# Asking for one part of a quarter's keys a block earlier, in a kernel that fills one queue with loads

## The chip, the core and the metric

The kernel runs on 1 core of one Trainium2 chip. What counts is the device time of one execution in microseconds (us), as the median of several runs. The engines are TensorE (PE in the profile: matmuls; PEld: its weight loads), VectorE (DVE), ScalarE (ACT), GpSimd (POOL) and SyncE (SP), which issues every DMA of this kernel on one queue.

## What is computed

For one sequence of 2048 rows and 512 columns the kernel computes a sliding-window attention with 32 heads of 16 columns and a dense layer with a gelu, and mixes the two by a gate:

```python
S, D, F, H, Dh, W = 2048, 512, 1792, 32, 16, 256
q, k, v = heads(x @ wqkv)
scores = einsum("bhqd,bhkd->bhqk", q, k) * Dh ** -0.5
mask = (idx[:, None] - idx[None, :] >= 0) & (idx[:, None] - idx[None, :] < W)
a = (softmax(where(mask, scores, -1e9)) @ v) @ wo
b = gelu(x @ w1 + b1) @ w2 + b2
g = sigmoid((x * gate_w).sum(-1, keepdims=True))
out = g * a + (1 - g) * b
```

## The kernel before, in words

The rows are cut into four quarters of 512 (T), a quarter into four blocks of 128 keys (NB = 4). The heads are worked on in eight groups of four. So attention runs over 8 x 16 = 128 blocks (NU), that is 32 quarters, one after the other. Every product is made of float32 values split into a high and a low part, hence three matmuls for one (`mm3`, L127 to L129).

First come the projections of all four quarters; their queries and keys go to DRAM (SQ and SK, in high and low parts). Then attention runs, interleaved on TensorE with the dense layer: the matmuls `u` (x times w1) and `y` (times w2) in eight pieces (`mlp`), and at the end `a` (times wo).

Attention has two passes, the second twelve blocks behind the first (LEAD = 12):

- The maxima. `att_max` (L667, its matmul is L680, called sm after its output) multiplies 64 queries of the tile `qd` with the 320 keys of the tile `kd` that their window covers, and VectorE takes the largest (L684). `kd` has two slots, for quarters in turn. A slot holds 256 + 512 keys: first the last 256 of the quarter behind (the old part), then the quarter's own 512 (the new part). Half block j of a quarter (j from 0 to 7) reads the 320 keys that end at 64(j+1) + 256.
- The scores. `att_exp` (L724, matmul L736, called st) multiplies keys in `ks` with queries in `qs`, and ScalarE takes the exponential (L765). At each quarter's end `att_pvs` multiplies with the values (L792, pv_sm and pv_st).

All loads go through `send` (L138), that is SP's queue, in the order in which the program text is run. `load_kd` (L639) sends the old part from SK of the quarter behind and the new part from SK of the quarter itself; `load_qd`, `load_ks` send three DMAs each, `load_qs` two, `att_load_v` one. SP runs its queue in order. A DMA is issued when the tile it overwrites has been read, when what it reads is written, and when the DMA eight issues before has landed, as eight semaphores go round.

The order of all instructions is written out by a planner in the kernel's own text. It keeps a clock with a cost for each step. `send` books 500 ns (ISSUE) of a line and one of eight lanes for 5 or 7 us (LOADS, SLOW); `arrive` (L149) marks a key such as ("qd", group, quarter) with the booked landing plus 1.2 us. `scores` (L1202) yields for each step the keys that it needs, and the loop behind it (L1249) then takes the attention step, or a matmul of the dense layer, by what is marked ready. The planner does not see the chip: where its clock is off, engines wait.

In `scores`, m counts the blocks of the maxima and u = m - 12 those of the scores. At the second step (i == 1) of the first block of a quarter (m % 4 == 0) the loads of the next quarter of maxima are asked for: `kd`, old part and new, then `qd`. In this same block, at its end, follow `ks` for the next quarter of scores (as 12 is a multiple of 4) and the values. `qs` is asked for at the end of the second block of a quarter of maxima at first, then at that of the third. The dense layer adds its own: `load_x` (L882) brings the next quarter of x as four DMAs called `mx`, in a tile (tag xt) of which there is one buffer; at the end of the first `u` the last quarter's x is stored from that tile (XT<-xt).

Of the kernel before, what the change touches and what calls it, by code (L numbers as in the profile page):

```python
# [19 lines left out]
NT = S // T  # L20
NB = T // 128
# [11 lines left out]
def gated_mix(ctx: ExitStack, tc: tile.TileContext, x, wqkv, wo, w1, b1, w2, b2, gate_w, out):  # L33
# [12 lines left out]
    def f32(ap):  # L46
        return ap.bitcast(F32)
# [90 lines left out]
    def send(to, by, ns=LOADS):  # L138

        nc.sync.dma_start(to, by)  # L140
        k = sent[0] = (sent[0] + 1) % 8
        at = max(line[0], now[0], lanes[k])
        line[0], lanes[k] = at + ISSUE, at + ns
# [5 lines left out]
    def arrive(key):  # L149

        mark(key, lanes[sent[0]] + MARGIN)

    def after(ns, fn, *args):
        now[1] += 1
        heapq.heappush(todo, (now[0] + ns, now[1], fn, args))
# [353 lines left out]
    def qkv(t):  # L509
# [38 lines left out]
        for n, (kind, j) in enumerate(pieces):  # L548
# [18 lines left out]
            if t == 2 and n in (1, 2):  # L567
                load_kd(0, n - 1)
# [25 lines left out]
    def repeat():  # L594

        t, j, to, by = twice.pop(0)
        send(to, by)
        mark(("twice", t, j))
# [3 lines left out]
    def slot(g_, c):  # L602
        return (g_ * NT + c) % 2

    def heads(st, g_):

        return st[g_ // 4][2 * (g_ % 4):2 * (g_ % 4) + 2]

    def ready(t, g_, k):
        need(*[(("qk", "twice")[g_ // 4], t, k * NC + 2 * (g_ // 4) + a) for a in range(2)])  # L610
# [5 lines left out]
    def load_ks(g_, c):  # L616


        ready(c, g_, 1)
        n = 2 * NB  # L620
        put_pairs([f32(ks[64 * s + 4:64 * s + 52, slot(g_, c)]) for s in range(2)], SK[c], g_)
        arrive(("ks", g_, c))

    def put_pairs(to, st, g_):

        n = 2 * NB
        for s in range(2):
            v = to[s].rearrange("r a x -> r (a x)")
            src = part(st, g_, s)
            if s:  # L630
                mid = v[:, 192:192 + 256 * (n - 1)].rearrange("r (n x) -> r n x", x=256)[:, :, 0:128]
                send(mid, src[:, 64:64 + 128 * (n - 1)].rearrange("r (n x) -> r n x", x=128), SLOW)
                ends = v.rearrange("r (n j) -> r n j", j=64)[:, 0:4 * n:4 * n - 1]
                send(ends, src.rearrange("r (n j) -> r n j", j=64)[:, 0:2 * n:2 * n - 1], SLOW)
            else:
                v = v.rearrange("r (n x) -> r n x", x=256)[:, :, 64:192]
                send(v, src.rearrange("r (n x) -> r n x", x=128), SLOW)

    def load_kd(g_, c):  # L639
        for t in range(max(c - 1, 0), c + 1):  # L640
            ready(t, g_, 1)
            k0 = 0 if t == c else T - W
            at = W if t == c else 0
            src = heads(SK[t], g_)[:, :, :, :, k0:].rearrange("s d u a c -> (s d u) a c")
            send(f32(kd[0:96, slot(g_, c), :, at:at + T - k0]), src, SLOW)

    def load_qd(g_, c):
        ready(c, g_, 0)
        put_pairs([f32(qd[48 * s:48 * s + 48, slot(g_, c)]) for s in range(2)], SQ[c], g_)
        arrive(("qd", g_, c))  # L650

    def load_qs(g_, c):
        ready(c, g_, 0)
        need(("v", NT - 2, NB - 1))
        for s in range(2):
            v = f32(qs[64 * s + 4:64 * s + 52, :, c * T:(c + 1) * T])
            send(v, part(SQ[c], g_, s).rearrange("r (a c) -> r a c", a=2))
        arrive(("qs", g_, c))

    def att_load_v(g_, c):  # L660
        need(*[("v", c, b) for b in range(NB)])
        vt = vbuf[:, c % 2]
        dst = vt[:, 0:NB * 68].rearrange("p (j c) -> p j c", c=34)
        send(dst, SV[c].rearrange("p j s c -> p (j s) c")[:, :, 34 * g_:34 * g_ + 34])
        vts[g_, c] = vt

    def att_max(g_, b, i):  # L667

        if b % RB == 0 and (g_, b // RB) not in Ms:
            Ms[g_, b // RB] = sb.tile([128, 2 * RB, 2], F32, tag="M", bufs=2, name=f"M{g_}_{b}")  # L670
        M = Ms[g_, b // RB]
        hb, pr = divmod(i, 2)
        c, n = b // NB, slot(g_, b // NB)
        j = 2 * (b % NB) + hb
        w = min(64 * (2 * b + hb + 1), W + 64)
        k1 = 64 * (j + 1) + W
        bank("sm", ("max", g_, b, i))
        p = ps.tile([128, 320], F32, tag="sm", bufs=3, name=f"sm{g_}_{b}_{i}")
        v = pairs(p[:, :w])
        nc.tensor.matmul(v, qd[0:96, n, pr, 128 * j:128 * (j + 1)], two(kd[0:96, n, pr, k1 - w:k1]),  # L680
                         start=True, stop=True)

        def red():
            nc.vector.tensor_tensor_reduce(v, v, two(mask[:, 320 - w:320]), 1.0, -3e38,  # L684
                                           ALU.add, ALU.max, M[:, 2 * (b % RB) + hb, pr:pr + 1])
        tick(max(w / 2.4 + 6, 110))
        put("V", w / 0.96 + 117, red, 130, 500, key=("max", g_, b, i))

    def att_rows(g_, rb):
        def turn():  # L690
            turn_of(g_, rb)

        def puts():
            for i in range(4):
                for hb in range(2):
                    put("G", 400, lambda i=i, hb=hb: put_rows(g_, rb, i, hb), PUT * (i + 0.5 * hb), 1500,
                        key=("rows", g_, rb) if i == 3 and hb else ("row", g_, rb, i, hb))
        put("V", 720, turn, 0, 1500, key=("turn", g_, rb), then=puts,
            req=[("v", NT - 2, NB - 1)] + [("max", g_, rb * RB + b, i) for b in range(RB) for i in range(4)])
# [18 lines left out]
    def rows_of(g_, kb, i):  # L718

        k0 = kb * 128 + i // 2 * 64  # L720
        w = min(W + 64, S - k0)
        return [("rows", g_, b) for b in range(kb // RB, (k0 + w - 1) // (RB * 128) + 1)]
# [47 lines left out]
    def blocks_of(kb):  # L770

        return list(range(max(kb - 5, 0), kb + 1))
# [422 lines left out]
    NU = NG * NKB  # L1195
# [6 lines left out]
    def scores():  # L1202

        for u in range(-LEAD, NU):
            m = u + LEAD
            gm, bm = divmod(m, NKB)
            step_ = STEP if u >= 0 else STEP0
            for i in range(4):
                if i == 1 and m % NB == 0 and NB <= m < NU - NB:
                    load_kd(*divmod(m // NB + 1, NT)), load_qd(*divmod(m // NB + 1, NT))  # L1210
                if i % 2 == 0:
                    pair = (i, i + 1) if stage[0] != "u" else (i,)
                elif len(pair) == 2:
                    continue
                else:
                    pair = (i,)
                for op, i in [(op, k) for k in pair for op in ORDER[:3]] + [("f", k) for k in pair]:
                    if op == "s" and u >= 0:
                        yield (rings["st"][0], ("ks", u // NKB, u % NKB // NB), *rows_of(u // NKB, u % NKB, i))
                        att_exp(u // NKB, u % NKB, i)  # L1220
                    if op == "m" and m < NU:
                        yield (rings["sm"][0], ("qd", gm, bm // NB))
                        att_max(gm, bm, i ^ XOR)
                    if op == "p" and i == PVAT and 1 <= u <= NU - LEAD and u % NB == 0:
                        g_, kb = divmod(u - 1, NKB)
                        yield (rings["st"][0], rings["sm"][0], *[("pt", g_, b, h) for b in blocks_of(kb) for h in (0, 1)])
                        att_pvs(u - 1)
                    if op == "f":
                        yield step_ / 4
            if m < NU and bm % RB == RB - 1:  # L1230
                att_rows(gm, bm // RB)
            if m % NB == QAT % NB and QAT <= m < QAT + NKB:
                load_qs(0, (m - QAT) // NB)
            if u > NU - LEAD and u % NB == 0:
                yield ()
                att_pvs(u - 1)
            if u % NB == 0 and NB <= u < NU - NB:
                load_ks(*divmod(u // NB + 1, NT))
            if u % NB == 2 and NB < u < NU - 3 * NB:
                load_qs(*divmod(u // NB + 3, NT))  # L1240
            if COPY[0] <= u < COPY[1] and u % 2 == 1 and twice:
                repeat()
            if u % NB == 0 and u >= 0:
                att_load_v(*divmod(u // NB, NT))
            if u - NU + NKB == YAT:
                for k in range(6):
                    after(1500 + YGAP * k, load_y, *divmod(k, 2))
# [94 lines left out]
```

## Time and profile before

| | |
|---|---|
| median of 3 runs | 703.48 us (703.24 to 703.89) |
| the profiled execution | 704.36 us |
| its span, first to last instruction | 702.4 us |
| TensorE busy | 691.5 us, 98% of the span |
| granted TensorE clock | 1.000 |
| first and last load of kd | at 80.9 and 585.0 us |

The profile is of one execution. Times in it count from the span's start. A chain of waits is followed back from the last instruction, at each step to what released it. A row of the timeline has start, length, engine, line (L140 is the issue in `send`), operation, out<-in and how many instructions of one kind follow one another; where several follow, the length takes in the waits between them. The waits view says who waited for whom: us in all, how often, the longest.

### The profile page before, as it was taken

To read this page: it belongs to the slowest core of one execution; us is meant where nothing else is said; L and a number is where in the kernel's file an instruction comes from. 1 tells how busy PE (TensorE), PEld (TensorE's weight loads), DVE (VectorE), ACT (ScalarE), POOL (GpSimd) and SP (SyncE) were. 2 spreads that over 40 slices of the span, in tenths; PEclk is the share of its full clock that TensorE was granted. 3 is DMA by queue.
4 is the path that set the end of the run, shared out by engine and by line. 5 is a ranking of instruction groups with operands and counts; after the bars stand their busy time and mean duration, and the time that the engine had idled before them with its cause. 6 is when DMAs were issued, how large, how long until landed. Compare 5 with 4: busy or idle time off the path is not lost.

```text
span 702.4 us, 17477 instructions
## 1 busy us (share of the span) xinstructions
PE 691.5 (98%) x6129; PEld 594.1 (85%) x6129; DVE 514.4 (73%) x1558; ACT 416.5 (59%) x972; POOL 364.9 (52%) x855
## 2 busy tenths in 40 slices
PE   8999999999899999999999999999999999999998
PEld 7888888888688888888888888888888888878886
DVE  4733326799769977986898799869878986984653
ACT  4434532369438845863696488449746954894641
POOL 4200000569756865786589667757865776630000
PEclk9999999999999999999999999999999999999999
DMA  9979698999898899799997799997999899757652
GB/s 309 367 229 386 201 403 244 287 315 249 218 265 189 211 286 246 176 234 256 293 229 186 219 247 220 248 271 176 253 244 241 178 220 293 204 167 219 201 201 100
DMA packets 178102, 169.97 MB, mean 242 GB/s; under 512 B 56544, under 2 KB 122848, under 8 KB 178016
## 3 DMA queue, kind: packets, MB, share of 16 engines
q1 hardware_dynamic: 178016, 168.87, 87.1%
q8 instruction: 48, 0.79, 0.5%
q14 instruction: 38, 0.31, 0.2%
HBM read 111.68 MB, written 61.34 MB: 246 GB/s over the span
## 4 chain that ended last, share of the span: by engine, by line
PE 85%; DMA 7%; DVE 2%; ACT 2%; issue 1%; POOL 1%; SPq 1%; POOLq 0%; DVEq 0%; ACTq 0%
PE sm L680 9%; PE st L736 8%; PE pv_sm L792 7%; PE y L127 6%; PE y L129 6%; PE y L128 6%; PE u L127 6%; PE u L128 5%; PE u L129 5%; PE qk L127 4%; PE qk L129 4%; PE qk L128 4%; PE a L127 2%; PE a L129 2%; PE a L128 2%; PE v L127 2%
## 5 line engine op out<-in xcount | busy, mean ns | idle before, releaser
L684 DVE CUSTOM_DVE_ANT_1 sm<-sm,mask 128x320 f32<-128x320 f32 (+4 forms) x512 | 230.4, 489 | 62.2 <-PE sm L680 58.2
L752 POOL TENSOR_SCALAR_AFFINE_SELECT pt<-pt 64x256 f32<-64x256 f32 (+1 forms) x538 | 208.9, 408 | 110.6 <-ACT pt L765 99.7
L765 ACT ACTIVATE pt<-st 128x320 f32<-128x320 f32 (+4 forms) x512 | 191.9, 427 | 108.3 <-PE st L736 105.0
L680 PE MATMUL sm<-kd,qd 96*128 96x320 f32 (+4 forms) x512 | 148.0, 304 | 1.0 <-DVE M L684 0.8
L736 PE MATMUL st<-qs,ks 128*128 128x320 f32 (+4 forms) x512 | 143.1, 297 | 2.9 <-DMA ks<-SK 1.7
L716 POOL CAST qs<-tt 4x256 fp32r<-4x256 f32 x256 | 123.9, 484 | 27.5 <-DVE tt L708 15.9
L680 PEld LDWEIGHTS sm<-kd,qd 96*128 96x128 f32 x512 | 96.8, 189 | 19.9 <-DVE M L684 5.7
L736 PEld LDWEIGHTS st<-qs,ks 128*128 128x128 f32 x512 | 97.3, 190 | 11.6 <-issue 2.3
L129 PE MATMUL y<-w2h,h 128*128 128x512 f32 x224 | 85.1, 380 | 0.8 <-DVE h L961 0.5
L127 PE MATMUL y<-w2h,h 128*128 128x512 f32 x224 | 85.1, 380 | 0.0
L128 PE MATMUL y<-w2l,h 128*128 128x512 f32 x224 | 84.8, 378 | 0.0
L127 PE MATMUL u<-mx,w1h 128*128 128x512 f32 x196 | 76.9, 393 | 0.2 <-DVE sqh L949 0.2
L129 PE MATMUL u<-mx,w1l 128*128 128x512 f32 x196 | 74.3, 379 | 0.0
L128 PE MATMUL u<-mx,w1h 128*128 128x512 f32 x196 | 74.2, 379 | 0.0
L792 PE MATMUL pv_sm<-pt,vbuf 64*32 64x320 f32 (+4 forms) x1408 | 73.3, 346 | 0.1
L792 PE MATMUL pv_st<-pt,vbuf 64*32 64x320 f32 (+4 forms) x1408 | 72.9, 346 | 0.0
L684 DVE DVE_READ_ACCUMULATOR2_ANT M<- 128x1 f32 x512 | 71.2, 139 | 0.0
L792 PEld LDWEIGHTS pv_sm<-pt,vbuf 64*32 64x32 f32 x1408 | 49.4, 106 | 22.2 <-issue 3.2
L456 DVE TENSOR_TENSOR qke<-qk,qke 128x512 fp32r<-128x512 f32 x32 | 22.1, 691 | 40.9 <-ACT qke L453 31.3
L453 ACT ACTIVATE qke<-qk 128x512 fp32r<-128x512 f32 x32 | 19.1, 598 | 51.5 <-PE qk L129 28.6
L129 PEld LDWEIGHTS y<-w2h,h 128*128 128x128 f32 x224 | 42.2, 188 | 7.3 <-DVE h L961 1.3
L473 POOL MEMSET vx<- 128x32 f32 x16 | 2.4, 154 | 85.9 <-DMA SQ<-qke 32.0
(165 smaller groups left out, 1331.8 us busy)
## 6 DMA issues: line engine op xcount, KB each, us to landing
kd<-SK SPq DMA_DIRECT2D x32, 384.0 KB
qs<-SQ SPq DMA_DIRECT2D x64, 192.0 KB
mx<-XT SPq DMA_DIRECT2D x24, 512.0 KB
SQ<-qke SPq DMA_DIRECT2D x16, 512.0 KB
SK<-qke SPq DMA_DIRECT2D x16, 512.0 KB
ND<-nd SPq DMA_DIRECT2D x32, 256.0 KB
raw_w<-in_B_w_dram SPq DMA_DIRECT2D x28, 256.0 KB
qd<-SQ SPq DMA_DIRECT2D x32, 192.0 KB
```

Source lines behind the costliest of these rows:

```text
L127: nc.tensor.matmul(p, lh, rh, start=first, stop=False)
L128: nc.tensor.matmul(p, lh, rl, start=False, stop=False)
L129: nc.tensor.matmul(p, ll, rh, start=False, stop=last)
L453: nc.scalar.activation(halves(e[:, h]), p, AF.Copy)
L456: nc.vector.tensor_sub(halves(e[:, 1 - h]), p, halves(f32(e[:, h])))
L680: nc.tensor.matmul(v, qd[0:96, n, pr, 128 * j:128 * (j + 1)], two(kd[0:96, n, pr, k1 - w:k1]), start=True, stop=True)
L684: nc.vector.tensor_tensor_reduce(v, v, two(mask[:, 320 - w:320]), 1.0, -3e38, ALU.add, ALU.max, M[:, 2 * (b % RB) + hb, pr:pr + 1])
L716: nc.gpsimd.tensor_copy(dst, src.unsqueeze(1).broadcast_to([4, 2, RB, 32]))
L736: nc.tensor.matmul(pairs(p[:, :w]), ks[:, slot(g_, kb // NB), pr, at:at + 128], two(qs[:, pr, k0:k0 + w]), start=True, stop=True)
L752: nc.gpsimd.affine_select(out=v, in_=v, pattern=[[0, v.shape[1]], [1 - 2 * e, 64]], compare_op=ALU.is_ge, fill=0.0, base=-e, channel_multi ...
L765: nc.scalar.activation(halves(pt[:, hf, pr, :w]), sorted_(p[:, :w]), AF.Exp, scale=SCALE)
L792: nc.tensor.matmul(pv[r // 64][32 * i:32 * i + 32, q - c * T:e - c * T], vts[g_, b // NB][r:r + 64, v:v + 32], rhs(r), start=start, stop=s ...
```

## The change

`load_kd` gets two switches for its two parts. The old part of quarter n + 2 is asked for in the last block of quarter n (m % 4 == 3), at the second step; the new part and `qd` stay where both parts and `qd` were, at the second step of the block that follows.

```diff
-    def load_kd(g_, c):
-        for t in range(max(c - 1, 0), c + 1):
+    def load_kd(g_, c, old=True, new=True):
+        for t in range(c - 1 if old and c else c, c + new):
             ready(t, g_, 1)
             k0 = 0 if t == c else T - W
             at = W if t == c else 0
...
             for i in range(4):
+                if i == 1 and m % NB == NB - 1 and m < NU - 2 * NB:
+                    load_kd(*divmod(m // NB + 2, NT), new=False)
                 if i == 1 and m % NB == 0 and NB <= m < NU - NB:
-                    load_kd(*divmod(m // NB + 1, NT)), load_qd(*divmod(m // NB + 1, NT))
+                    load_kd(*divmod(m // NB + 1, NT), old=False), load_qd(*divmod(m // NB + 1, NT))
```

The first quarter of each group has no quarter behind it and so no old part.

## The prediction

> **What bounds the kernel now.** I read the page of the profile first, then who TensorE waited for, then the SyncE (SP) queue around the one large wait, and last the DMA engines' share there.
>
> ```profile
> span 702.4 us, 17477 instructions
> ...
> PE 691.5 (98%) x6129; PEld 594.1 (85%) x6129; DVE 514.4 (73%) x1558; ACT 416.5 (59%) x972; POOL 364.9 (52%) x855
> ```
>
> TensorE is busy for 691.5 of 702.4 us, so everything that is not a matmul can give back at most 702.4 - 691.5 = 10.9 us, over the whole span. The change adds and removes no matmul. The second full resource is the DMA, in the view of its queues and issues:
>
> ```profile
> DMA packets 178102, 169.97 MB, mean 242 GB/s; under 512 B 56544, under 2 KB 122848, under 8 KB 178016
> ...
> q1 hardware_dynamic: 178016, 168.87, 87.1%
> ...
> kd<-SK SPq DMA_DIRECT2D x24, 192.0 KB
> ```
>
> One queue's packets take 87.1% of the 16 engines' span; the old parts of `kd` are 24 transfers of 192 KB in it. The change moves loads, so the question is whether a load ends any of those 10.9 us. The view of waits, kept to TensorE, answers it:
>
> ```profile
> engine line waited for: us in total, times, longest us
> PE st L736 <- DMA ks<-SK: 1.7, 1, 1.7
> PE warm0.0_188 L506 <- POOL idle L57: 1.2, 1, 1.2
> ...
> PE st L736 <- ACT nd L812: 0.8, 1, 0.8
> PE sm L680 <- DVE M L684: 0.8, 2, 0.5
> ```
>
> One DMA stands in it: once, for 1.7 us, a score matmul (st) waited for the load of `ks`. The matmuls of the maxima (sm), which are the readers of `kd`, waited for VectorE only. The same from the other side, the view of the tile `kd`:
>
> ```profile
> L140 SPq DMA_DIRECT2D kd<-SK x56: 540/569/2288, 80.9 to 585.0; - x56
> ...
> its engine sat idle before it (us, times) until:
>   DVE M L684: 6.5, 21
>   issue: 4.3, 22
> ```
>
> Before 512 weight loads and 512 matmuls on `kd`, no idle time ended with the landing of a `kd` or `qd` load. So the transfer that is moved is on no path today. Its first-order worth is nil, and what is left are side effects: on the loads behind it in SP's queue, on the full DMA engines, and on the order that the planner writes.
>
> **The change part by part.** Calls first. `scores` asks for the old part at every m = 3, 7, ... up to 119 (30 calls); the seven that belong to quarter 0 of a group have no old part and issue nothing. So 23 DMAs are moved, one to a quarter, each by one block of keys; none is added or removed, bytes are the same.
>
> *SP's issue slots.* At the median of 569 ns from the row above, 23 x 0.569 = 13.1 us of issuing leave the bursts at the quarters' starts and stand elsewhere in the same queue. In sum SP does the same. What that frees depends on whether SP was the late one at the burst. Two places show both answers; first a quarter in the steady state, then the narrow window inside its pair of `kd` loads:
>
> ```profile
> 227.95 5.17 SPq L140 DMA_DIRECT2D kd<-SK  x2
> 233.17 1.76 SPq L140 DMA_DIRECT2D qd<-SQ  x3
> 235.03 1.72 SPq L140 DMA_DIRECT2D ks<-SK  x3
> ```
>
> ```profile
> 232.58 0.55 SPq L140 DMA_DIRECT2D kd<-SK  x1
> ```
>
> The columns are start, length, what. The old part goes out at 227.95; the new part only at 232.58, and between them SP stands for about 232.58 - 227.95 - 0.57 = 4.1 us, because the new part overwrites keys that the quarter's last maxima still read. The old part's own region, the first 256 keys, is read by the first two blocks of a quarter only (the window of half block j ends at 64(j+1)+256 and is 320 wide, so it leaves these keys from j = 4 on). It has no such wait, neither here nor one block sooner. Here the old part's slot is covered by the wait that follows; taking it away lets `qd` and `ks` start at the same 233.17 and 235.03. Worth 0.
>
> The change adds no wait for TensorE at the new place: at block 3 of the quarter the readers, blocks 0 and 1, are done by a whole block. What SP can meet there is the landing of the DMA eight issues back, since eight semaphores go round:
>
> ```profile
> SPq L140 <- DMA kd<-SK: 29.5, 31, 1.8
> ```
>
> Such waits for a `kd` load come to 29.5 us in 31 places, none over 1.8 us. They are moved with it rather than removed: the queue holds eight whatever their order. Queued behind the moved issue are then the parts of `mx`, `ya`, `ND` and the copies of SQ and SK that fall between the block and the quarter's end, and after them the new part of `kd`, `qd` and `ks`. Who waits for those: TensorE for none of the first kind (no row of the waits above), so up to 1.8 us plus a 0.57 us slot is hidden there by loads that land before they are needed. If that cover is gone, the bill is those 2.4 us at one place.
>
> *The one place where a load ends the wait of TensorE.* The chain that ended last runs through it:
>
> ```profile
> 164.94 7.08 DMA kd<-SK
> 172.04 7.75 DMA XT<-xt
> ...
> 182.31 4.29 DMA ks<-SK
> 186.60 0.09 issue
> 186.69 0.37 PE st L736
> ```
>
> and SP's queue over the same time:
>
> ```profile
> 160.95 3.26 SPq L140 DMA_DIRECT2D qs<-SQ  x2
> 164.31 0.53 SPq L140 DMA_DIRECT2D raw_w<-in_B_w_dram  x1
> 164.94 1.45 SPq L140 DMA_DIRECT2D kd<-SK  x2
> 166.44 1.75 SPq L140 DMA_DIRECT2D qd<-SQ  x3
> 168.85 4.39 SPq L140 DMA_DIRECT2D XT<-xt  x4
> 179.94 0.32 SPq L140 DMA_DIRECT2D mx<-XT  x1
> 180.31 2.46 SPq L140 DMA_DIRECT2D ks<-SK  x3
> ```
>
> To be read: the old part of `kd` issues at 164.94 and lands at 172.02; it is the eighth before the fourth store of `xt`, which therefore goes out at 172.04 and lands at 179.79; the first part of `mx` overwrites `xt`, so SP stands until 179.94; `ks` stands behind `mx` in the queue, lands at 186.60, and the matmul starts at 186.69. At first sight the moved load begins this chain, and its early departure should pull all of it forward. But how far can it go? One block sooner in the queue puts it behind the two `qs` (asked at the end of the block two before), so its issue can start at 160.95 + 3.26 = 164.21 at the soonest, not at 164.94: 0.73 us. And the fourth store then waits for another of the same four predecessors (two `qs`, the weight, the old part), which go through the same engines. Those were full:
>
> ```profile
> 160.00:165.00 5.00, 5.00 (x29) 4.28 (x28) 5.00 (x20) 5.00 (x13) 4.74 (x9) 1.00 1.10 188
> 165.00:170.00 5.00, 5.00 (x57) 4.26 (x63) 4.86 (x20) 5.00 (x14) 4.78 (x11) 1.00 1.07 241
> 170.00:175.00 5.00, 5.00 (x75) 4.35 (x59) 5.00 (x11) 4.78 (x11) 4.60 (x10) 1.00 1.11 320
> ```
>
> The last two columns are the DMA engines' share and GB/s. At 1.10, 1.07 and 1.11 the engines have no gap, and a permutation of what waits in front of them ends at the same moment. So this term lies between -0.73 us (the whole shift arrives) and 0 (only the order changes); it could be above 0 only by the planner's order, which is priced below. I take 0, by the shares.
>
> [...]
>
> *The planner's clock.* `send` books 500 ns of line per issue (ISSUE, L143) and one of eight lanes for 7 us (SLOW); `arrive` marks `qd` and `ks` from these. With one issue fewer in the burst these marks come about one ISSUE sooner, more where a lane was booked out. From the second quarter on the order of dense and attention matmuls on TensorE can therefore differ, by a matmul here and there. That costs nothing by itself, as TensorE has the same work and 98% fill. It is unknown in sign: the waits of TensorE beside the startup are 0.8 us and less apiece, so I bound the sum by one wait of the largest size seen, 1.7 us, each way.
>
> *The sum.* 0 (slots) + 0 (kd's own readers) + 0 (the chain at 186.69, bound -0.73) + 0 (order, bounds -1.7 and +1.7). The profiled execution took 704.36 us, its span 702.4 and 1.96 around it, and is 0.88 above the median of the runs, 703.48; the change comes out as a difference of 0, so the forecast is **703.5 us** by the median. A measurement of this kernel can tell about 0.2%, 1.4 us, from no change.
>
> **The rivals.**
>
> *The load does not really go sooner.* SP is late at many bursts (at 164 us it works off a backlog: 3.26 us for two `qs`), so an instruction placed one block sooner leaves the chip a few tenths sooner. For it: the 0.73 us above. Against: in the steady quarter SP passes the old part at 227.95, well ahead of the new one, so there it is on time. The result is also 703.5 us.
>
> *The wait at 186.69 goes.* If the planner's earlier marks put `ks` ahead of the `xt` stores and `mx`, or more dense matmuls ahead of that st, TensorE no longer stands there: 703.48 - 1.73 = 701.8 us. The 1.73 is this row's:
>
> ```profile
> 186.69 0.37 PE L736 MATMUL st<-qs,ks 128*128 128x320 f32 x1 [1.73 <-DMA ks<-SK]
> ```
>
> For it: it is the only wait for a load, and the moved DMA is in its chain. Against: the chain's middle, the stores and the 7 us of SP behind them, has nothing to do with `kd`, and it would need 1.4 of 1.73 us to go where I find at most 0.73.
>
> *A longer wait at a quarter's first st (slower).* The planner now believes that `ks` lands sooner; the chip, with full DMA engines, does not land it sooner. Where the mark of `ks` decides when attention goes on, the st comes sooner in TensorE's order, with fewer dense matmuls ahead of it, and TensorE, which runs in order, stands for the rest. In the place above the st is at the landing already, so each dense matmul that changes to behind it adds its own time, 0.22 us by the step of this chain:
>
> ```profile
> 157.60 0.22 PE u L127
> ```
>
> From seven of them on (7 x 0.22 = 1.5 us) it is a measurable loss; with eight, 1.7 us (703.48 + 1.7), the result is 705.2 us. For it: the boundary has no slack, and nothing on the chip holds the planner to the truth. Against: the mark moves by about 500 ns, which is two or three such matmuls, unless a booked lane adds to it.
>
> **How the numbers follow.** Forecast (moved, covered) 0.38; not really sooner 0.14; both within 0.2%, together 0.52. The wait goes 0.24, at 701.8. A new or longer wait 0.24, at 705.2. The range takes in both side cases' centres, since leaving either out leaves more than 2 in 10 outside: 701.7 to 705.3; it leaves about 0.2 for tails beyond. The likeliest case's own range is 702.7 to 704.4. Chances: faster 0.24, same 0.52, slower 0.24.
>
> **What would show it right or wrong.** In the changed kernel the pair of `kd` loads at a quarter is one, the other stands about a block (some 4 us) sooner; TensorE's busy time stays at 691 to 692 us; the waits of TensorE for VectorE and ScalarE stay near today's; sm still waits for no DMA. The forecast holds by its reasons if the wait of st for `ks` near 187 us is there again within 0.7 us of 1.7, and no second DMA stands in the view of TensorE's waits. It is wrong towards faster if that row is gone and the idle time of TensorE is down from 10.9 to about 9; wrong towards slower if a row for `ks`, `kd`, `qd` or `mx` of over a microsecond has come.

## The result

The changed kernel takes 710.73 us by the median (710.31 to 713.04), the kernel before 703.68 us beside it. The ratio is 1.011, with a 95% interval of 1.0091 to 1.013: it is slower by 7 us, outside the range of the forecast. Beside the experiments below the kernel before took 700.5 to 709.0 us, with medians of 702.45 to 703.65, so each run there is told by its ratio to the kernel before beside it, with the 95% interval. The profiled execution of the changed kernel took 713.04 us. Its page and its longest waits of TensorE:

```profile
span 710.6 us, 17479 instructions
...
PE 695.5 (98%) x6129; PEld 597.1 (84%) x6129; DVE 518.7 (73%) x1560; ACT 417.7 (59%) x972; POOL 361.1 (51%) x853
```

```profile
engine line waited for: us in total, times, longest us
PE sm L680 <- DVE M L684: 4.0, 5, 2.1
PE y L129 <- DVE h L961: 2.2, 2, 1.2
PE u L127 <- DVE sqh L949: 2.1, 3, 0.9
PE warm0.0_188 L506 <- POOL idle L57: 1.2, 1, 1.2
PE st L736 <- ACT nd L812: 0.9, 1, 0.9
```

Two rows of the kernel before that go with it:

```profile
PE u L127 <- DVE sqh L949: 0.6, 2, 0.4
PE y L129 <- DVE h L961: 0.5, 1, 0.5
```

The span grew by 8.2 us (702.4 to 710.6): idle time of TensorE from 10.9 to 710.6 - 695.5 = 15.1 us, and its busy time by 4.0 us. No DMA stands in TensorE's waits any more: the row of `ks` is gone. The three rows for VectorE (sm, y and u) were 1.9 us before and are 8.3 us now, each for the result of a matmul that VectorE has not yet read or finished. So no load holds TensorE up in this execution, and it is worse off.

The load itself left sooner, but mostly by less than a block. SP's queue at the quarter shown before, first the row that stood just ahead of the pair of `kd` loads at 227.95 in the kernel before, then the changed kernel:

```profile
227.26 0.59 SPq L140 DMA_DIRECT2D SK<-SK  x1
```

```profile
231.58 0.55 SPq L140 DMA_DIRECT2D kd<-SK  x1
232.17 0.60 SPq L140 DMA_DIRECT2D SK<-SK  x1
237.06 0.55 SPq L140 DMA_DIRECT2D kd<-SK  x1
237.65 1.76 SPq L140 DMA_DIRECT2D qd<-SQ  x3
239.51 1.71 SPq L140 DMA_DIRECT2D ks<-SK  x3
```

The old part leaves at 231.58, 5.5 us ahead of the new one. But in the kernel before it was 232.58 - 227.95 = 4.6 us ahead already: SP had come to it early, so here the old part only changes places with one copy of SK and gains 0.9 us. Over the 23 moved loads its lead on the new part grew from 0.7 us to 3.1 us at the median. The new part waits for TensorE as it did before (4.3 us, before 4.1). `qd` and `ks` follow the new part with the same spacing as before. The `kd` readers of the changed kernel:

```profile
L140 SPq DMA_DIRECT2D kd<-SK x56: 539/552/1195, 81.3 to 595.0; - x56
...
its engine sat idle before it (us, times) until:
  DVE M L684: 14.4, 26
  issue: 3.8, 19
```

Idle time that VectorE ended has grown from 6.5 to 14.4 us (weight loads and matmuls together), and still none of it ends with a load.

Where the time went shows in two stretches, taken from the table of busy times. Columns: stretch, its length, busy time of TensorE, its weight loads, VectorE, ScalarE and GpSimd, then the granted clock, the DMA share and GB/s. Before:

```profile
130.00:200.00 70.00, 66.86 (x493) 57.27 (x493) 58.73 (x193) 43.21 (x96) 51.46 (x101) 1.00 0.98 261
340.00:450.00 110.00, 109.58 (x1126) 92.31 (x1125) 98.08 (x311) 79.73 (x186) 81.56 (x184) 1.00 0.92 229
```

After:

```profile
130.00:200.00 70.00, 64.93 (x469) 54.83 (x468) 55.47 (x177) 40.41 (x88) 47.68 (x91) 0.98 0.87 245
340.00:450.00 110.00, 106.55 (x1032) 90.67 (x1036) 100.07 (x317) 80.42 (x187) 80.33 (x180) 1.00 0.90 223
```

Between 130 and 200 us, where the scores begin, TensorE is idle for 5.1 us and not 3.1; between 340 and 450 us for 3.4 us and not 0.4. In the second stretch the kernel before left TensorE next to no gap while VectorE was busy for 89% of the time. A part of the 8.2 us is the clock, an estimated 1.7 us: in this execution TensorE's granted clock was about 0.50 for 3.4 us (last section).

### The profile page after: what moved, and what is told of

Same layout as the page of the kernel before. It is cut to its first block, busy times and chain, and to the rows that moved or that the text cites. A ratio compares the mean times of both kernels' runs of the same rounds, so it can differ in the third digit from the quotient of the medians.

```text
span 710.6 us, 17479 instructions
## 1 busy us (share of the span) xinstructions
PE 695.5 (98%) x6129; PEld 597.1 (84%) x6129; DVE 518.7 (73%) x1560; ACT 417.7 (59%) x972; POOL 361.1 (51%) x853
## 5 line engine op out<-in xcount | busy, mean ns | idle before, releaser
L752 POOL TENSOR_SCALAR_AFFINE_SELECT pt<-pt 64x256 f32<-64x256 f32 (+1 forms) x538 | 204.9, 401 | 124.1 <-ACT pt L765 113.3
L716 POOL CAST qs<-tt 4x256 fp32r<-4x256 f32 x256 | 126.9, 496 | 26.7 <-DVE tt L708 15.2
L943 ACT ACTIVATE x1h<-u,b1c 128x512 f32<-128x512 f32 x56 | 38.7, 691 | 17.3 <-PE u L129 17.0
```

Source lines behind the costliest of these rows:

```text
L716: nc.gpsimd.tensor_copy(dst, src.unsqueeze(1).broadcast_to([4, 2, RB, 32]))
L752: nc.gpsimd.affine_select(out=v, in_=v, pattern=[[0, v.shape[1]], [1 - 2 * e, 64]], compare_op=ALU.is_ge, fill=0.0, base=-e, channel_multi ...
L943: nc.scalar.activation(halves(x1), sorted_(p), AF.Identity, bias=b1c[:, f:f + 1])
```

## The experiments

First, whether the load or the order costs the time. Then, what makes one order dearer than another: how full VectorE is (theory V), the marks that the planner sees later (theory M), or any lasting reshuffle, whatever sets it off (theory R).

**Load or order?** Two kernels take the change apart. `send` gets a switch for the DMA and one for the booking; the moved call and a call at the old place use one each.

```diff
-    def send(to, by, ns=LOADS):
-        nc.sync.dma_start(to, by)
+    def send(to, by, ns=LOADS, dma=True, book=True):
+        if dma:
+            nc.sync.dma_start(to, by)
+        if not book:
+            return
...
# sp_only: the DMA a block sooner, the booking at the old place
+                    load_kd(*divmod(m // NB + 2, NT), new=False, book=False)
+                    load_kd(*divmod(m // NB + 1, NT), new=False, dma=False)
# plan_only: the booking a block sooner, the DMA at the old place
+                    load_kd(*divmod(m // NB + 2, NT), new=False, dma=False)
+                    load_kd(*divmod(m // NB + 1, NT), new=False, book=False)
```

The four compute engines of sp_only have instruction for instruction the order of the kernel before, those of plan_only that of the changed kernel.

> The old part is issued a block sooner on the chip, as in the changed kernel, but the planner books it where it was before; so TensorE, VectorE, ScalarE and GpSimd run the order of the kernel before and only SP's queue is changed. Theory P (the loss comes from the planner's order, because its bookings changed): 703.7 us within 1.4. Rival Q (the loss comes from the load itself, earlier in SP's full queue and on full DMA engines): about 710.7 us.

> The reverse: the planner books the old part a block sooner, as in the changed kernel, but SP issues it where it was before; the four compute engines run the order of the changed kernel. Theory P: about 710.7 us. Rival Q: 703.7 us within 1.4.

Measured: sp_only 704.23 us, ratio 1.0014 (0.9989 to 1.0038); plan_only 712.46 us, ratio 1.0113 (1.008 to 1.0146). The waits of TensorE in plan_only (its line numbers stand three higher):

```profile
PE sm L683 <- DVE M L687: 4.5, 7, 2.1
PE u L127 <- DVE sqh L952: 2.2, 3, 0.9
PE y L129 <- DVE h L964: 2.2, 2, 1.2
```

These are the rows of the changed kernel again, 8.9 us, with every load where it was before. The loss is in the order that the planner wrote; moving the load alone makes no difference that can be measured.

**Which part of the order?** The change made whole, but only for the quarters whose old place is the boundary m = 4 or m = 8 (2 loads), or only from m = 16 on (21 loads by these conditions, not the 20 of the expectation: 2 and 21 make the 23).

```diff
# early_only (late_only: 16 <= m + 1, 16 <= m)
-                if i == 1 and m % NB == NB - 1 and m < NU - 2 * NB:
+                if i == 1 and m % NB == NB - 1 and m < NU - 2 * NB and m + 1 < 16:
...
-                    load_kd(*divmod(m // NB + 1, NT), old=False), load_qd(...)
+                    load_kd(*divmod(m // NB + 1, NT), old=not m < 16), load_qd(...)
```

> The change made whole (issue and booking), but only for the quarters whose loads fall before the scores begin (quarters 2 and 3; 2 of the 23 moved loads), where the planner's eight lanes are booked out. Theory P: the maxima of the third quarter are marked ready 5 us later there, so most of the 7 us comes back: 707 to 711 us. Rival Q: 2 of 23 of the loss, about 704.3 us, or more if the queue's fullness there decides.

> The change made whole, but only for the later quarters (from the sixth on; 20 of the 23 moved loads). Theory P: the late bookings find free lanes, so little moves: 703.5 to 706 us. Rival Q: 20 of 23 of the loss, about 709.8 us.

Measured: early_only 707.95 us, 1.0063 (1.0037 to 1.0088); late_only 707.06 us, 1.0047 (1.0029 to 1.0064), above what I expected of it. The two add up to the 1.1%. The two stretches tell them apart; early_only:

```profile
130.00:200.00 70.00, 64.65 (x476) 54.60 (x475) 56.02 (x179) 40.97 (x90) 47.95 (x91) 1.00 0.89 253
340.00:450.00 110.00, 109.37 (x1130) 92.81 (x1130) 97.99 (x315) 80.98 (x188) 81.72 (x184) 1.00 0.97 234
```

late_only:

```profile
130.00:200.00 70.00, 67.52 (x498) 58.05 (x497) 59.33 (x194) 43.25 (x97) 52.14 (x103) 1.00 0.98 266
340.00:450.00 110.00, 106.69 (x1106) 90.14 (x1106) 98.81 (x310) 78.90 (x182) 81.18 (x182) 1.00 0.90 225
```

The early loads open the gap of 5.3 us in the first stretch and leave the second whole (0.6); the late ones leave the first (2.5) and open the second (3.3). The changed kernel has both, and the orders say why: from about 230 us on, TensorE's order in early_only is again, matmul for matmul, that of the kernel before, and its order in the changed kernel is that of late_only. So the loss has two parts, one from a passing change of the order and one from a lasting one.

What the early loads do to the planner can be read off its arithmetic. While the projections still store, all eight lanes are booked ahead; the old part, sent earlier, takes a lane in front of others, and on the planner's clock the queries of the third quarter are marked 2.0 us later (138.6 instead of 136.6) and those of the fourth 5.0 us later (155.1 instead of 150.1). It then holds the maxima back and writes matmuls of the dense layer alone, until they run out of ready inputs. (The expectation of early_only put the 5 us on the third quarter.) On the chip this is the longest wait of the changed kernel:

```profile
160.22 0.69 DVE L949 SCALAR_TENSOR_TENSOR sqh<-u,x1h 128x512 f32<-128x512 f32 x1 [0.38 <-ACT u L946]
160.32 0.38 PE L129 MATMUL u<-xt,w1l 128*128 128x512 f32 x1
160.83 0.68 DVE L961 TENSOR_TENSOR h<-x1h,h 128x512 fp32r<-128x512 f32 x1
...
161.61 0.71 DVE L955 SCALAR_TENSOR_TENSOR x1h<-sqh,x1h 128x512 f32<-128x512 f32 x1
...
162.24 0.48 DVE L684 CUSTOM_DVE_ANT_1 sm<-sm,mask 128x320 f32<-128x320 f32 x1
...
162.84 0.40 PE L680 MATMUL sm<-kd,qd 96*128 96x320 f32 x1 [2.14 <-DVE M L684]
```

Three maxima had been written by 159.9, which fills the three buffers of the sm ring (`bufs=3`, L678); the first reduction that frees one, at 162.24, stands in VectorE's queue behind three steps of the gelu (160.22, 160.83 and 161.61), and TensorE stands from 160.70 to 162.84.

**Is it VectorE's load?** Since VectorE ends these waits and is the fullest engine beside TensorE (busy for 73% of the span), I made its reductions short, in both orders.

```diff
-            nc.vector.tensor_tensor_reduce(v, v, two(mask[:, 320 - w:320]), 1.0, -3e38,
+            nc.vector.tensor_tensor_reduce(v[:, 0:32], v[:, 0:32], two(mask[:, 320 - w:320])[:, 0:32], 1.0, -3e38,
```

> The kernel before, with the maxima taken over the first 64 of each 320 products alone: 496 of the 512 VectorE instructions of the maxima become shorter (489 ns to some 200), the planner's bookings and the order of every engine stay. It leaves out most of the comparison in the maxima (any lower bound serves the exponential as well). It is the base for the next run. Theory V (the changed order costs because TensorE waits for VectorE where VectorE is full): 699 to 702 us, the waits for VectorE shrink. Rival O (TensorE's order costs by itself or by ScalarE's chains): 702.5 to 704 us.

> The changed kernel with the same shorter VectorE instructions, order and bookings of the changed kernel. Theory V: most of the 7 us between the two is gone, at most 2.5 us over the run with the light maxima and the order before. Rival O: still 5 us or more over it.

Measured: light_before 698.53 us, 0.9931 (0.9903 to 0.9958); light_after 706.24 us, 1.0035 (1.0018 to 1.0052). Both gain (light_before falls even below the 699 us of theory V), but the distance between the two orders is 7.7 us, as large as before. So theory V falls: how much VectorE has to do is not what sets the price of the order. In light_after the same wait stands at the same place:

```profile
159.50 0.63 ACT L952 ACTIVATE sqh<-sqh 128x512 f32<-128x512 f32 x1 [0.22 <-DVE sqh L949]
...
160.16 0.71 DVE L955 SCALAR_TENSOR_TENSOR x1h<-sqh,x1h 128x512 f32<-128x512 f32 x1
160.79 0.22 DVE L684 CUSTOM_DVE_ANT_1 sm<-sm,mask 128x64 f32<-128x64 f32 x1
...
161.13 0.40 PE L680 MATMUL sm<-kd,qd 96*128 96x320 f32 x1 [1.87 <-DVE M L684]
```

The reduction is 0.22 us long and still comes behind the gelu's step at 160.16, which reads what ScalarE finishes at 160.13. It is a matter of which instruction stands behind which.

**Are the late marks the cause?** One mark alone was moved, without any load, and in the changed kernel marks were put back. `arrive` (L149) adds a number for a named key.

```diff
-        mark(key, lanes[sent[0]] + MARGIN)
+        mark(key, lanes[sent[0]] + MARGIN + SHIFT.get(key, 0.0))
# mark_qd:     the kernel before,  {("qd", 0, 2): 2000.0}
# mark_ks:     the kernel before,  {("ks", 0, 2): -500.0}
# ks_late:     the kernel before,  {("ks", 0, 2): 3000.0}
# qd3_back:    the changed kernel, {("qd", 0, 3): -5000.0}
# qd3_ks_back: the changed kernel, {("qd", 0, 3): -5000.0, ("ks", 4, 2): -2000.0}
```

q3_only is the change made whole for the fourth quarter alone, by the same conditions as early_only.

> The kernel before with one number changed: the planner's mark for the queries of the third quarter of maxima comes 2.0 us later, as it does in the changed kernel. No load is moved and no booking changed. Theory P, in its narrow form (this late mark starves the maxima and starts the loss): 705.5 to 708.5 us, as with the early quarters alone. Rival: the loss there needs the later landing times of the other loads as well: 703.7 us within 1.4.

> The change made whole for one quarter alone, the fourth (1 of the 23 moved loads); no mark of queries is changed by it at first, only landings booked behind. Theory P: small, 702.5 to 705 us. Rival (any moved booking reshuffles the order and costs, wherever it is): 705 to 708 us.

> The changed kernel whole, with one mark put back: that of the queries of the fourth quarter of maxima comes 5.0 us sooner, which takes out the delay that the moved bookings gave it. Theory M (the late mark holds the maxima back, the matmuls of the dense layer then run alone and TensorE waits for their gelu chain and later for bunched maxima): the waits between 140 and 200 us shrink to those of the kernel before, the later half of the loss stays: 706 to 708 us. Rival (any changed order costs about as much): 710 us or more, as the changed kernel.

> As qd3_back, with a second mark put sooner by 2.0 us: that of the keys of the third score quarter of the fifth group, at which the planner of the changed kernel holds the scores back with no dense matmul ready. Theory M: another 1 to 2 us back, 704.5 to 706.5 us. Rival: no better than qd3_back.

> The kernel before with one mark 0.5 us sooner: that of the keys of the third score quarter, whose landing TensorE waits for. No load is moved. Four score and maxima matmuls change places with three dense ones, and the order comes together again behind. My slower rival on record says: the wait at 187 us grows by the 0.65 us of those three matmuls, 704.3 us. Rival (any changed order costs 2 to 4 us): 706 us or more.

> The kernel before with the same mark 3.0 us later, nearer to what the chip does there. If the wait of 1.7 us for the keys can be filled with dense matmuls: 701.8 to 702.5 us, and the row of that wait is gone. Rival (the maxima are held back with the scores and the time is lost elsewhere): 703.5 to 705 us.

Measured: mark_qd 707.41 us, 1.0048 (1.0027 to 1.007); q3_only 706.07 us, 1.0029 (1.0008 to 1.005); qd3_back 707.40 us, 1.0087 (1.0069 to 1.0105); qd3_ks_back 708.62 us, 1.0104 (1.0082 to 1.0125); mark_ks 703.79 us, 1.0019 (0.9998 to 1.004); ks_late 703.03 us, 1.0018 (1.0 to 1.0036).

One number in the planner, no load moved, costs as much as the twenty-one late loads. q3_only, with one load moved and no mark of queries changed at first, lies in the range of its rival and not in that of theory P. And mark_qd does not cost where I thought. The stretches of mark_qd:

```profile
130.00:200.00 70.00, 68.01 (x499) 58.17 (x498) 59.05 (x196) 42.92 (x96) 52.65 (x101) 1.00 0.99 265
340.00:450.00 110.00, 105.75 (x1105) 90.22 (x1105) 96.77 (x307) 78.64 (x184) 81.08 (x181) 1.00 0.89 217
```

The first stretch, where the late mark works, has even less idle time than before (2.0 us); the loss is 200 us further on (4.3). And qd3_back, which clears the first stretch (70 - 66.91 = 3.1 us idle), keeps 3.4 in the second:

```profile
130.00:200.00 70.00, 66.91 (x492) 57.42 (x491) 59.12 (x192) 43.03 (x96) 51.17 (x99) 1.00 1.01 273
340.00:450.00 110.00, 106.57 (x1106) 90.10 (x1106) 98.83 (x309) 79.39 (x185) 80.93 (x182) 1.00 0.90 223
```

So theory M holds for the first stretch and not for the whole. How much time came back can't be told closely: the ratio fell from 1.011 to 1.0087, and the two intervals overlap. From about 212 us on the order of qd3_back is that of late_only, and the profiled spans of the two are the same, 705.1 us. The second mark put back brought nothing. mark_ks and ks_late cost 0.2%, at most 0.4%, which can't be told from nothing. Their order comes together again with that of the kernel before, after some 330 and 115 matmuls. But that alone does not make a change free: the order of early_only comes together again too, after some 570 matmuls, and it costs 0.6%, with TensorE idle for 2.3 us between 160 and 164 us (the fence in the last section). The wait for `ks` is gone from the view of waits in ks_late, and its median, between its two ranges, shows no gain.

**Or does any lasting change of the order cost?** Three constants of the planner were changed by 1% and 4%, no load moved; and the kernel before was compared with itself.

```diff
# slow7070 / loads5050 / margin1250, each alone in the kernel before
-SLOW = 7000.0
+SLOW = 7070.0
-LOADS = 5000.0
+LOADS = 5050.0
-MARGIN = 1200.0
+MARGIN = 1250.0
```

> The kernel before once more, unchanged, as one of the compared kernels: it shows what the comparison makes of no difference at all, and a second profile shows whether the wait for the keys at 187 us comes every time. All theories: ratio 1.000 within 0.003.

> The kernel before with one constant of the planner changed by 50 ns (MARGIN, 1200 to 1250); no load is moved; the order is the same up to about 295 us and another one behind. Theory R (the order before is a lucky or well-chosen one, and any lasting reshuffle by the same planner costs): 704.5 to 708 us. Theory M (only marks that come microseconds late cost): 703.5 us within 1.4.

> The kernel before with another constant changed by 1% (SLOW, 7000 to 7070); no load is moved; the order differs from about 150 us on. Theory R: 704.5 to 708 us. Theory M: 703.5 us within 1.4.

> The kernel before with a third constant changed by 1% (LOADS, 5000 to 5050); no load is moved; the order is, but for a dozen places, the one that moving the fourth quarter's load alone gave (1.0029). Theory P and R: the same time as that one, 704.5 to 707 us. If the moved load itself was at work there: 703.5 us within 1.4.

Measured: before_again 703.02 us, 0.9995 (0.9978 to 1.0012); margin1250 704.05 us, 1.0019 (0.9997 to 1.004); slow7070 708.49 us, 1.008 (1.0063 to 1.0097); loads5050 705.41 us, 1.0045 (1.003 to 1.0059). A change of a constant by 1% that means nothing for the chip costs 5.5 us. An estimated 1.8 us of that is the clock: it was granted at 0.997 or 0.998 in all four executions of slow7070 (0.0025 x 708). slow7070 lies above the range of theory R, loads5050 in it, margin1250 below it and in that of theory M. The second stretch of these, before_again first, then slow7070, loads5050 and margin1250:

```profile
340.00:450.00 110.00, 110.00 (x1133) 93.63 (x1131) 99.17 (x316) 80.36 (x188) 83.34 (x186) 1.00 0.93 234
```

```profile
340.00:450.00 110.00, 106.96 (x1038) 90.86 (x1043) 97.67 (x310) 79.05 (x184) 80.25 (x179) 0.98 0.88 219
```

```profile
340.00:450.00 110.00, 107.18 (x1116) 92.23 (x1115) 97.65 (x309) 78.82 (x184) 83.37 (x184) 1.00 0.90 223
```

```profile
340.00:450.00 110.00, 107.42 (x1117) 91.73 (x1115) 96.54 (x306) 79.44 (x182) 79.25 (x182) 1.00 0.94 230
```

Idle: 0.0, 3.0, 2.8 and 2.6 us. Every run that has the order of the kernel before in this stretch, early_only among them, has 0.0 to 0.8 us of idle time there. Every run with another order and the reductions at full length has 2.6 to 4.3 us. These are four other orders, though, and not ten: that of the changed kernel, which late_only, plan_only and the two with marks put back share (but for some 70 matmuls in one of them), one of mark_qd, q3_only and loads5050 (the same but for five matmuls from about 188 us on), and one each of slow7070 and margin1250. That a mark, a moved load and a constant lead to the same order and to ratios of 1.0048, 1.0029 and 1.0045 says again that the order costs, whatever sets it off.

Theory R is borne out for three of these four orders; margin1250 has the idle time in this stretch, but its time can't be told from that of the kernel before. So most of the lasting changes tried cost time, that any would is not shown, and early_only shows that a passing one can cost too. Why the order of the kernel before fits in this stretch better than the others was not tried. That the order was chosen for it is not shown either. The planner's own count of time without work does not tell: it is 5.9 us for the kernel before, 9.0 for the changed one, but 5.2 for loads5050 and 6.1 for slow7070.

## Why the prediction was wrong, point by point

- *The readers of `kd` wait for no load; the move is worth nothing by itself; SP's slots, its eight outstanding DMAs and the full DMA engines pay nothing for it.* Right: sp_only, 1.0014 (0.9989 to 1.0038). The likeliest case's own range began at 702.7 us, 0.8 us under the median of 703.48; no run shows a gain of that size from the moved load: the median of sp_only is 0.8 us above that of the kernel before beside it (704.23 and 703.41), which can't be told from nothing.
- *The old part of the pair stands about a block (some 4 us) sooner.* Half right. At the median its lead grew by 2.4 us (0.7 to 3.1); at the quarter at 227.95, where SP was said to be on time, by 0.9 us only (4.6 to 5.5), because there it had left early before.
- *The wait of st for `ks` stays.* Wrong, without weight. It is gone in the changed kernel, in a second profile of the kernel before it is 0.8 us and not 1.7, and in the profile of sp_only it is 0.7 us at most (two waits, 1.0 us together). A size taken from a single execution was used as if it belonged to the kernel. Nor did its removal in ks_late show in the median.
- *The planner's clock.* This is the step that failed, twice. "With one issue fewer in the burst these marks come about one ISSUE sooner, more where a lane was booked out": two marks came 2.0 and 5.0 us later, since the moved booking took a lane ahead of others where all eight were booked out. And: "That costs nothing by itself, as TensorE has the same work and 98% fill", bounded by "one wait of the largest size seen, 1.7 us, each way". The measured term is 7 us (plan_only, with no load moved: 1.0113). The bound was taken from the waits that the order before happens to have; a different order has waits of its own, as the 2.14 us at 162.84. The 98% were a property of that order, not of the work: a reshuffle could win 10.9 us at most, and nothing in the profile bounded what it could lose.
- *The slower rival.* It had the right sign and the wrong mechanism: a mark that comes sooner, and a longer wait for `ks`. mark_ks moved that mark sooner: in its profile TensorE is busy for 4.00 of the 4 us from 183 to 187, where the wait for `ks` had stood, and its ratio is 1.0019 (0.9998 to 1.004). What came in the changed kernel were waits for VectorE, at other places.
- *The fence of the DMA share at 160 to 175 us* was read for its last two columns. The same rows show TensorE at 5.00 of 5 and VectorE at 4.86 to 5.00 of 5: a stretch in which TensorE has no idle time to take up a delay.

## What to carry to other kernels

Where a program's order is computed from booked costs, an edit to one booking can be an edit to the order of every engine. Price the reshuffle first, and by runs: change a constant of the planner by 1% and see what that alone does. Compare a step with the planner held still (issue here, book there) before judging it, and do not take the fill of the present order, or its largest wait, for a bound on what another order may cost.

## What the runs showed of the hardware that was not expected

TensorE's granted clock fell to about half for 3.4 us in the profiled execution of the changed kernel, 164 us into the span of 710.6. Around the 2.14 us wait:

```profile
160.00:164.00 4.00, 1.75 (x9) 1.05 (x7) 3.68 (x10) 3.53 (x9) 2.91 (x5) 1.00 1.15 202
164.00:168.00 4.00, 4.00 (x15) 3.45 (x14) 2.90 (x11) 2.89 (x7) 1.56 (x4) 0.57 0.76 190
```

The last but two is the granted clock: 0.57 over 4 us, in rows of 0.4 us 0.90 from 164.0, 0.50 from 164.4 to 167.6, 0.84 from there to 168.0 and 1.00 behind. The shortfall, 0.43 x 4, gives an estimate of 1.7 us lost. The matmuls of `u` start 0.43 us apart there, and 0.22 us apart just before the wait. The same stretch of early_only, where TensorE is idle as long (2.3 us of the first 4):

```profile
160.00:164.00 4.00, 1.74 (x9) 1.06 (x8) 3.91 (x11) 3.53 (x8) 2.73 (x4) 1.00 1.10 191
164.00:168.00 4.00, 4.00 (x24) 3.60 (x23) 4.00 (x17) 4.00 (x11) 2.89 (x7) 1.00 0.70 212
```

There the clock stays at 1.00. In mark_ks it fell to 0.57 over 4 us, behind a stretch in which TensorE was idle for 1 us of 4 and waited for no more than 0.5 us at a time:

```profile
175.00:179.00 4.00, 3.02 (x17) 2.05 (x15) 4.00 (x14) 3.05 (x9) 3.75 (x8) 1.00 0.27 108
179.00:183.00 4.00, 4.00 (x13) 3.34 (x13) 3.25 (x12) 1.57 (x4) 3.79 (x9) 0.57 1.05 263
```

So the clock fell behind 1 us of idle time in 4 in mark_ks, and stayed at 1.00 behind 2.3 us in 4 in early_only. It fell more often in one order than in the other: a granted clock of 0.998 or less was recorded in 18 of 28 executions of the kernels that start in the changed order and have a gap of about 2 us there (the changed kernel, plan_only, early_only, light_after), against 16 of 104 in the order of the kernel before (with before_again and sp_only) and none of 9 in late_only. What decides it is not shown.
